# Shifted fp16 terms with GpSimd adds in place of every third VectorE exp pair of an attention and feed-forward kernel

## The chip, the cores and the metric

The kernel runs on one core of one Trainium2 chip. The metric is the device time of one execution in microseconds (us), median over runs. The engines are PE (TensorE; PEld is its weight load), ACT (ScalarE), DVE (VectorE), POOL (GpSimd) and SP, which issues the DMAs. All fast runs of one kernel here lie within 1.5% of each other, and all runs used below were in the fast state, except the two single runs that only price instructions, whose state is unknown.

## The reference, cut to what matters

```python
xn = layernorm(x)                                  # x: 1 x 2048 x 512, bf16
q = xn @ wq  (32 heads of 16);  k = xn @ wk;  v = xn @ wv   # one k and v for all heads
p = softmax(q @ k.T / 4)                           # 32 x 2048 x 2048 scores
s = (p @ v) @ wo
g = silu((silu(xn @ w_gate) * (xn @ w_up)) @ w_down)
return x + s * g
```

The exps dominate: 32 x 2048 x 2048 of them, in 1024 tiles of 128 x 1024.

## The kernel before

The kernel computes transposed scores into three PSUM slots of 128x1024 ("ring"), takes exps from two slots on ScalarE and from the third on VectorE, and multiplies them by the values into one accumulating PSUM bank ("o_ps"). Each engine's order of instructions is laid down at build time by a planner in the kernel, which simulates the engines with a duration for each operation. At run time each engine works strictly in that order and waits on semaphores.

VectorE's way to an exp needs no table. A score, scaled so that one unit is 1/1024 of an octave, is written as a uint16 whose bits, read as fp16, are a number near the exp (linear between powers of two). Two score tiles make a pair. A three-instruction tail turns the pair into two better terms, each with a value matmul of its own:

```python
# first pass, one for each of the two tiles; reads PSUM
pa = OP("DVE", 1.135, [...], nc.vector.tensor_scalar(out=Ub[ui][:, x*1024:(x+1)*1024], in0=ring[2][:],
        scalar1=ubias, scalar2=UINF, op0=ALU.add, op1=ALU.min))
# ... (cut: bookkeeping of the pair)
o1 = OP("DVE", 0.6, ..., out=Wb, in0=Ub, 0x3FF, 0x3800, bitwise_and, bitwise_or)      # mask
o2 = OP("DVE", 0.6, ..., out=Eb, in0=Ub, 0x7C00, bitwise_and)                         # exponent
o3 = OP("DVE", 1.135, ..., tensor_tensor(out=Wb, in0=Wb, in1=Ub, op=mult))            # product
# two value matmul groups per pair: Eb with VD[0], Wb with VD[1]
```

The second argument of `OP` is the planner's duration. Code is cut and shortened here.

Of the kernel before, what the change touches and what calls it, by code (L numbers as in the profile page):

```python
# [1 line left out]

# [8 lines left out]
FP16 = mybir.dt.float16  # L11
# [14 lines left out]
COFF = 4.0  # L26
CE, CW = 0.66858732, 0.66372796 * 1.0
DEN_LO = 16.0
# [5 lines left out]
PB_URG, AHEAD, LAZY, ACTMIN, ACTLOW = 6, 16, 8, 1.7, 1.5  # L34
TOL, MERGE = 0.12, 0.1

# [145 lines left out]
class _Sched:  # L182
    LAT = {"PE": 0.205, "ACT": 0.22, "DVE": 0.25, "POOL": 0.16, "DMA": 0.0, "EXT": 0.0}
    SAME = {"PE": 0.0, "ACT": 0.0, "DVE": 0.1, "POOL": 0.05, "DMA": 0.0}
    SWITCH = 0.105
    HOT = 0.3

    def __init__(self):
        self.free = {"PE": 0.0, "ACT": 0.0, "DVE": 0.0, "POOL": 0.0, "DMA": 0.0}
        self.ready = {e: [] for e in self.free}  # L190
        self.done = []
        self.pe_log = []
        self.seq = 0
        self.mode = None
        self.key = lambda o: o.prio
# [31 lines left out]
    def switch(self, mode):  # L227
        return self.SWITCH if self.mode is not None and mode != self.mode else 0.0

    def pick(self, e):  # L230
        lst = self.ready[e]
        if not lst:
            return None
        if e == "DMA":
            op = min(lst, key=lambda o: (o.ready, o.seq))
            return op.ready, op
        t = self.free[e]
        tm = max(t, min(o.ready for o in lst))
        now = [o for o in lst if o.ready <= tm + 1e-9]
        best = min(now, key=lambda o: (self.key(o), o.seq))  # L240
        if e == "DVE":
            hot = [o for o in lst if o.ready > tm and self.key(o)[0] < 1.6 and self.key(o) < self.key(best)]
            if hot:
                h = min(hot, key=lambda o: (o.ready, o.seq))
                fit = [o for o in now if tm + o.dur <= h.ready + self.HOT]
                best = min(fit, key=lambda o: (self.key(o), o.seq)) if fit else h
        return max(t, best.ready), best

    def place(self, op, start):
        e = op.eng  # L250
        op.start = start
        if e == "PE":
            op.start += self.switch(op.mode)
            self.mode = op.mode
        op.end = op.start + op.dur
        if e != "DMA":
            self.free[e] = op.end
        self.done.append(op)
        if e == "PE":
            self.pe_log.append(op)  # L260
        for u in op.users:
            u.left -= 1
            if u.left == 0:
                self._arm(u)
# [7 lines left out]
def kernel(  # L272
# [79 lines left out]
    vf = sb([P, NT, DH], FP32, "vf")  # L352
    VD = sb([P, 2, NT, 3 * DH], FP16, "VD")
    stats = sb([P, NT, nc.vector.BN_STATS_DIM], FP32, "stats")
    mv = sb([P, NT, nc.vector.BN_AGGR_DIM], FP32, "mv")
# [4 lines left out]
    QB = [sb([P, 512], BF16, f"QB{i}") for i in range(2)]  # L360
    NPB, NU, NE = 8, 3, 2
    Pb = [sb([P, 1024], BF16, f"Pb{i}") for i in range(NPB)]
    XB = [g2_sb[:, 2 * i:2 * i + 2, :].rearrange("p n d -> p (n d)") for i in range(NT // 2)]
    Ub = [sb([P, 2048], U16, f"Ub{i}") for i in range(NU)]
    Eb = [sb([P, 2048], U16, f"Eb{i}") for i in range(NE)]
    Wb = [sb([P, 2048], U16, f"Wb{i}") for i in range(NE)]
    th = [sb([P, 512], FP32, f"th{i}") for i in range(1)] * 2
# [120 lines left out]
    MMF = 0.215  # L488
    NBLK = NSC * NQ * 2
    NTILE = NBLK * NT * 2  # L490
    NPAIR = NSC * NQ
# [14 lines left out]
    def pro_x(c, pr, banks, ev_eng):  # L506
# [3 lines left out]
        for n0 in range(4 * c, 4 * c + 4, step):  # L510
# [22 lines left out]
            for n in range(n0, n0 + step):  # L533
                xo = OP("DVE", 0.33, [r, xr_rel[n % 4]], lambda n=n: e_xn(n), (pr - 0.15 if c == 0 else pr - 0.05, n),
                        name="xn")
                bk = banks[n % 4 // pk]
                h = n % pk
                t_ = OP("PE", 0.26, [xo, brel[bk]] + grp, lambda n=n, bk=bk, h=h: e_tr(n, bank[bk], h), (pr, n), "f",
                        "tr")
                xr_rel[n % 4] = t_  # L540
                grp = grp + [t_]
                if len(grp) == pk:
                    ee = ev_eng if n not in (1, 3) else "DVE"
                    ev = OP(ee, 0.5 if ee == "ACT" else 0.34 if pk == 1 else 0.6, grp,
                            lambda n=n, bk=bk, ee=ee: e_txe(n + 1 - pk, pk, bank[bk], ee), (pr - 0.1, n), name="txe")
                    if c:
                        held.append((grp[0], ev, bk))
                    grp = []
                    brel[bk] = ev
                    evs.append(ev)  # L550
# [24 lines left out]

    held = []
    evs = pro_x(0, 0.3, ("0a", "0b", "1a", "1b"), "ACT")
# [20 lines left out]
    for c in range(1, NSC):  # L598
# [7 lines left out]
        pro_v(c, evs, "2a", 0.7 + 0.01 * c)  # L606
    d_gate = [brel["2a"], brel["2b"], brel["m"]]

    m_rel = [brel["m"]]
# [63 lines left out]
    def e_out_add(n, src, eng):  # L673
        r = res[n % 4]
        return eng.tensor_tensor(out=r[:, :D], in0=src[:, :D], in1=x_sb[:, n, :], op=ALU.add)

# [3 lines left out]
    def g_out(n):  # L680
# [6 lines left out]
        m_rel[0] = m_  # L687
        ad = OP("POOL", 1.3, [m_, xr_rel[n % 4]], lambda: e_out_add(n, ab[i], nc.gpsimd), (0,), name="oadd")
        ab_rel[i] = ad
# [75 lines left out]
    unp = [[[], []] for _ in range(NBLK)]  # L765
    cur = {"ba": 0, "lastx": 1, "nA": 0, "exp": None, "pair": None, "np": 0, "issued": 0, "lastsc": None, "junk": 0, "nX": 0}
    slot = [None, None, None]
    pb_rel, w_rel, e_rel, wop_rel = [], [], [], []
    open_block(0)
# [126 lines left out]

    def act_sc(i, b, x, start):
        sc, t = place_sc(i, b, x, start, MMF)
        cur["lastx"] = x
# [11 lines left out]
        if k >= NPB:  # L911
# [3 lines left out]
                (1,), name="exp")  # L915
        cur["exp"] = ex
        slot[i] = ex
        unp[b][x].append((ex, k, t, buf))
# [16 lines left out]

    def dve_sc(b, x, start, dur):
        sc, t = place_sc(2, b, x, start, dur)
        first = cur["pair"] is None
        u = cur["np"]
        ui = u % NU  # L940
        pa = OP("DVE", 1.135, [sc, wop_rel[u - NU] if u >= NU else None],
                lambda: nc.vector.tensor_scalar(out=Ub[ui][:, x * 1024:(x + 1) * 1024], in0=ring[2][:], scalar1=ubias,  # L942
                                                scalar2=UINF, op0=ALU.add, op1=ALU.min), (1.5, u), name="passA")
        slot[2] = pa
        if first:
            cur["pair"] = (b, x, t, pa)
            return
        _, x0, t0, pa0 = cur["pair"]
        cur["pair"] = None
        cur["np"] += 1  # L950
        pair_blk.append(b)
        half = b % 2
        tx = {x0: t0, x: t}
        ei = u % NE
        o1 = OP("DVE", 0.6, [pa, pa0, w_rel[u - NE] if u >= NE else None], lambda: nc.vector.tensor_scalar(  # L955
            out=Wb[ei][:], in0=Ub[ui][:], scalar1=0x3FF, scalar2=0x3800, op0=ALU.bitwise_and,
            op1=ALU.bitwise_or), (2, u, 0), name="dM")
        o2 = OP("DVE", 0.6, [pa, pa0, e_rel[u - NE] if u >= NE else None], lambda: nc.vector.tensor_scalar(  # L958
            out=Eb[ei][:], in0=Ub[ui][:], scalar1=0x7C00, scalar2=None, op0=ALU.bitwise_and), (2, u, 1), name="dE")
        o3 = OP("DVE", 1.135, [o1, o2], lambda: nc.vector.tensor_tensor(  # L960
            out=Wb[ei][:].bitcast(FP16), in0=Wb[ei][:].bitcast(FP16), in1=Ub[ui][:].bitcast(FP16), op=ALU.mult),
            (2, u, 2), name="dW")
        wop_rel.append(o3)
        for i, (buf, o, rel) in enumerate(((Eb[ei], o2, e_rel), (Wb[ei], o3, w_rel))):
            mms = []
            dps = [o, oev[b - 1]]
            for g in range(4):
                tt = tx[g // 2]
                mms += mm_of(VD[:, i], lambda g, buf=buf: buf[:].bitcast(FP16)[:, g * 512:(g + 1) * 512], tt, half, (g,))
                dps.append(v_ready[tt // 4][i + 1])  # L970
            pv = OP("PE", MMF, dps, pv_emit(b, mms), (1, b, cur["nA"]), "c", "dpv")
            rel.append(pv)
            blk_pv[b].append(pv)
        check_done(b)
# [10 lines left out]
    LB = NBLK - 1  # L985
    LN = 4 * (NSC - 1)

# [99 lines left out]
    def pe_pick():  # L1087
# [42 lines left out]
        if tm is not None:  # L1130
            if ts is None or tm + sd.switch(co.mode) + co.dur <= ts + TOL:
                cands.append(tm)
            else:
                tm = None
        if td is not None and (ts is None or td + sd.switch("r") + MMF <= ts):
            if tm is None or td < tm - 0.2:
# [31 lines left out]
    def pe_do(start, what):  # L1168
# [20 lines left out]
        if kind == "dve":  # L1189
            dve_sc(arg[0], arg[1], start, MMF)  # L1190
            return
# [16 lines left out]
        if dt is not None and tile_ready(*dt) is not None:  # L1208
            at = max(sd.free["PE"], sd.avail(slot[2], "PE"), tile_ready(*dt))
            dve_sc(dt[0], dt[1], at, 0.015 if dt[1] != x else MMF)  # L1210

# [118 lines left out]
```

## Time and profile before

| | before |
|---|---|
| time, median | 788.7 us (786.6 to 790.0, 3 runs) |
| ACT busy, of a span of 786.6 us | 757.7 us, 96% |
| DVE busy | 740.2 us, 94% |
| PE busy | 723.8 us, 92% |
| POOL busy | 48.7 us, 6% |
| exps on ACT / first passes on DVE / tails on DVE | 778 / 246 / 123 |

From the page of the kernel before, the busy time of each engine and the groups of instructions that matter. The columns of a group are: line, engine, operation, output and input, form, count, then busy time and mean ns of one, then the engine's idle time just ahead of them and who ended it.

```profile
PE 723.8 (92%) x8097; PEld 218.6 (28%) x8098; DVE 740.2 (94%) x925; ACT 757.7 (96%) x864; POOL 48.7 (6%) x59
...
L914 ACT ACTIVATE Pb<-ring 128x1024 bf16<-128x1024 f32 x770 | 729.5, 1171 | 9.3 <-PE ring L856 8.6
L856 PE MATMUL ring<-QB,KT 32*128 32x512 bf16 x2048 | 319.0, 382 | 41.9 <-ACT Pb L914 35.3
L942 DVE TENSOR_SCALAR Ub<-ring 128x1024 uint16<-128x1024 f32 x246 | 299.3, 1217 | 12.3 <-PE ring L856 7.4
L960 DVE TENSOR_TENSOR Wb<-Wb,Ub 128x2048 f16<-128x2048 f16 x123 | 151.1, 1229 | 0.0
L958 DVE TENSOR_SCALAR Eb<-Ub 128x2048 uint16<-128x2048 uint16 x123 | 87.2, 714 | 0.0
```

Three engines are over 90% busy, and shares alone do not say which one bounds the kernel. Two stretches in mid-kernel do (the stretch and its length in us; then the busy us of PE, PEld, DVE, ACT and POOL in this order, with the number of instructions in brackets; then granted PE clock, DMA share, GB/s):

```profile
400.00:500.00 100.00, 92.29 (x1030) 27.78 (x1029) 98.29 (x118) 99.97 (x115) 7.18 (x6) 1.00 0.06 15
500.00:600.00 100.00, 93.79 (x1072) 27.22 (x1070) 95.95 (x112) 99.81 (x114) 2.98 (x2) 1.00 0.06 14
```

ACT has hardly a gap, DVE and PE have small ones. The waits agree (waiting us in total, times, longest):

```profile
ACT Pb L914 <- PE ring L856: 8.6, 13, 1.5
PE ring L856 <- ACT Pb L914: 35.3, 97, 1.0
```

ACT waited 8.6 us in the whole run for scores; PE waited four times that for ACT. So ACT is the bound, with DVE and PE close behind it.

### The profile page before, as it was taken

The numbers are of one execution on the slowest core, as the hardware profiler recorded it, in microseconds if no ns is written. First come the engines' busy times: TensorE is split into PE (matmuls) and PEld (weight loads), VectorE is DVE, ScalarE is ACT, GpSimd is POOL, SyncE is SP. The second block draws the span as 40 slices with busy tenths as digits, with TensorE's granted clock in tenths as the row PEclk, the third lists the DMA queues.
The fourth block names the chain that finished last, engine by engine and source line by source line (L and its number), as shares of the span: only waits on it lengthen the run. The fifth ranks groups of instructions, "written<-read, shape, count | busy, mean of one in ns | idle before, by whom it ended". The sixth has DMA issues, their size and how long they took to land.

```text
span 786.6 us, 19520 instructions
## 1 busy us (share of the span) xinstructions
PE 723.8 (92%) x8097; PEld 218.6 (28%) x8098; DVE 740.2 (94%) x925; ACT 757.7 (96%) x864; POOL 48.7 (6%) x59
## 2 busy tenths in 40 slices
PE   8999899999999899999999999989999999999995
PEld 3332232222222222222222222222222222222221
DVE  7678999999899999999999999999999999999997
ACT  6899899999999999999999999999999999999993
POOL 2100000000011000001002000000001100000001
PEclk9999999999899999999999999999999999999998
DMA  9300000000000000000000000000001000000001
GB/s 328 116 3 7 17 3 23 2 9 15 2 23 29 23 2 3 22 2 23 2 10 29 15 23 2 10 15 9 17 2 29 23 22 3 4 20 2 23 2 32
DMA packets 19464, 18.50 MB, mean 24 GB/s; under 512 B 8552, under 2 KB 15464, under 8 KB 19368
## 3 DMA queue, kind: packets, MB, share of 16 engines
q1 hardware_dynamic: 17496, 16.37, 6.9%
q8 instruction: 65, 1.06, 0.6%
q10 hardware_dynamic: 1872, 0.82, 0.4%
q14 instruction: 31, 0.25, 0.1%
HBM read 12.62 MB, written 2.34 MB: 19 GB/s over the span
## 4 chain that ended last, share of the span: by engine, by line
PE 36%; ACT 33%; DVE 20%; issue 9%; DMA 1%; SPq 0%; POOL 0%; ACTq 0%; DVEq 0%
ACT Pb L914 27%; PE ring L856 15%; PE m_ps L474 13%; PE o_ps L726 7%; DVE Ub L942 7%; ACT th L637 4%; DVE Wb L960 4%; DVE Eb L958 3%; DVE Wb L955 2%; ACT th L654 1%; DVE hT L643 1%; DVE ab L639 1%; DVE oa L739 1%; DMA dn<-oa 1%; DMA x_sb<-in_A_x_dram 0%
## 5 line engine op out<-in xcount | busy, mean ns | idle before, releaser
L914 ACT ACTIVATE Pb<-ring 128x1024 bf16<-128x1024 f32 x770 | 729.5, 1171 | 9.3 <-PE ring L856 8.6
L856 PE MATMUL ring<-QB,KT 32*128 32x512 bf16 x2048 | 319.0, 382 | 41.9 <-ACT Pb L914 35.3
L942 DVE TENSOR_SCALAR Ub<-ring 128x1024 uint16<-128x1024 f32 x246 | 299.3, 1217 | 12.3 <-PE ring L856 7.4
L856 PEld LDWEIGHTS <-KT 32*128 32x128 bf16 x2048 | 106.3, 90 | 349.7 <-issue 345.0
L960 DVE TENSOR_TENSOR Wb<-Wb,Ub 128x2048 f16<-128x2048 f16 x123 | 151.1, 1229 | 0.0
L726 PE MATMUL o_ps<-Pb,VA 128*32 128x512 bf16 x1540 | 149.1, 387 | 0.1
L958 DVE TENSOR_SCALAR Eb<-Ub 128x2048 uint16<-128x2048 uint16 x123 | 87.2, 714 | 0.0
L955 DVE TENSOR_SCALAR Wb<-Ub 128x2048 uint16<-128x2048 uint16 x123 | 86.0, 700 | 0.3 <-PE o_ps L726 0.2
L474 PE MATMUL m_ps<-xnT,wg_sb 128*32 128x512 bf16 x896 | 74.0, 384 | 0.8 <-DVE g_sb L656 0.3
L474 PE MATMUL m_ps<-wd_sb,hT 128*32 128x512 bf16 x896 | 73.4, 391 | 0.0
L474 PE MATMUL m_ps<-xnT,wu_sb 128*32 128x512 bf16 x896 | 70.7, 388 | 0.9 <-DVE ab L639 0.8
L711 POOL TENSOR_TENSOR oT<-oa,rb 128x512 bf16<-128x512 f32 x15 | 21.3, 1420 | 607.6 <-DMA rb<-dscr 267.8
L726 PEld LDWEIGHTS <-VA 128*32 128x32 bf16 x1556 | 38.6, 94 | 54.6 <-issue 53.8
L726 PE MATMUL o_ps<-Eb,VD 128*32 128x512 f16 x492 | 48.3, 386 | 2.6 <-DVE Eb L958 2.2
L726 PE MATMUL o_ps<-Wb,VD 128*32 128x512 f16 x492 | 48.8, 386 | 1.8 <-DVE Wb L960 1.2
L637 ACT ACTIVATE th<-m_ps 128x512 f32<-128x512 f32 x56 | 42.4, 758 | 0.0
L726 PEld LDWEIGHTS <-VD 128*32 128x32 f16 x984 | 29.0, 93 | 43.2 <-issue 41.2
L643 DVE TENSOR_TENSOR hT<-ab,m_ps 128x512 bf16<-128x512 f32 x56 | 38.1, 680 | 2.4 <-PE m_ps L474 2.1
L639 DVE SCALAR_TENSOR_TENSOR ab<-th,m_ps 128x512 f32<-128x512 f32 x56 | 38.0, 678 | 1.5 <-ACT th L637 1.0
L474 PEld LDWEIGHTS <-wg_sb 128*32 128x32 bf16 x896 | 17.2, 94 | 26.9 <-issue 26.3
L474 PEld LDWEIGHTS <-wu_sb 128*32 128x32 bf16 x896 | 16.4, 95 | 26.7 <-issue 24.5
L739 DVE COPY oa<-o_ps 128x512 f32<-128x512 f32 (+1 forms) x33 | 22.0, 668 | 1.5 <-PE o_ps L726 1.5
(106 smaller groups left out, 245.8 us busy)
## 6 DMA issues: line engine op xcount, KB each, us to landing
rb<-dscr SPq DMA_DIRECT2D x15, 256.0 KB
dn<-oa SPq DMA_DIRECT2D x120, 2.0 KB, 1.7
oa<-oa SPq DMA_DIRECT2D x60, 32.0 KB, 2.0
wg_sb<-in_B_w_gate_dram SPq DMA_DIRECT2D x1, 1792.0 KB, 12.1
wu_sb<-in_B_w_up_dram SPq DMA_DIRECT2D x1, 1792.0 KB
wd_sb<-in_B_w_down_dram SPq DMA_DIRECT2D x1, 1792.0 KB, 20.0
out_dram<-xn SPq DMA_DIRECT2D x14, 128.0 KB, 2.0
x_sb<-in_A_x_dram SPq DMA_DIRECT2D x3, 512.0 KB
```

The lines of the kernel that those rows point to most:

```text
L474: return [nc.tensor.matmul(out=dst[GRP * j:GRP * j + GRP, :], lhsT=w[:, GRP * j:GRP * j + GRP], rhs=rhs, start=start, stop=stop, tile_posi ...
L637: t_ = OP("ACT", 0.477, [a], lambda: nc.scalar.activation(out=th[i][:], in_=m_ps[:], func=ACT.Tanh, scale=0.5), (0,), name="tanh")
L639: s_ = OP("DVE", 0.6, [t_, ab_rel[i]], lambda: nc.vector.scalar_tensor_tensor(out=ab[i][:], in0=th[i][:], scalar=1.0, in1=m_ps[:], op0=ALU ...
L643: h = OP("DVE", 0.6, [b], lambda: nc.vector.tensor_tensor(out=hT[:, f, :], in0=ab[i][:], in1=m_ps[:], op=ALU.mult), (1,), name="hmul")
L726: r.append(nc.tensor.matmul(out=o_ps[GRP * g:GRP * g + GRP, :], lhsT=lhs, rhs=rhs, start=(n == 0), stop=(n == pv_total[(b, g)] - 1), tile_ ...
L739: oev[b] = sd.new(_Op("DVE", 0.6, [], lambda: [nc.vector.tensor_copy(out=oat[:, a:z], in_=o_ps[:, a:z]) for a, z in cuts], (0.2,), name="o ...
L856: return lambda: [nc.tensor.matmul(out=ring[sl][:, u * 512:(u + 1) * 512], lhsT=KT[half][GRP * g:GRP * g + GRP, t * P:(t + 1) * P], rhs=QB ...
L914: lambda: nc.scalar.activation(out=buf, in_=ring[i][:], func=ACT.Exp, scale=escale, bias=ebias),
L942: lambda: nc.vector.tensor_scalar(out=Ub[ui][:, x * 1024:(x + 1) * 1024], in0=ring[2][:], scalar1=ubias, scalar2=UINF, op0=ALU.add, op1=AL ...
L955: o1 = OP("DVE", 0.6, [pa, pa0, w_rel[u - NE] if u >= NE else None], lambda: nc.vector.tensor_scalar(out=Wb[ei][:], in0=Ub[ui][:], scalar1 ...
L958: o2 = OP("DVE", 0.6, [pa, pa0, e_rel[u - NE] if u >= NE else None], lambda: nc.vector.tensor_scalar(out=Eb[ei][:], in0=Ub[ui][:], scalar1 ...
L960: o3 = OP("DVE", 1.135, [o1, o2], lambda: nc.vector.tensor_tensor(out=Wb[ei][:].bitcast(FP16), in0=Wb[ei][:].bitcast(FP16), in1=Ub[ui][:]. ...
```

## The change

The intent is to free VectorE, so that it can take more exp tiles from ScalarE, by using idle GpSimd. Every third pair has no tail. Instead the first pass is followed on POOL by three adds of 256, 512 and 768 to the uint16 bits, a quarter octave each; the four fp16 numbers, weighted in the values by powers of 2^(-1/4), sum to a good exp. The pair then needs four value matmul groups instead of two. To find room, seven scratch buffers and eight rows of x that are dead after the layer norm form one pool of nine, other x rows hold the new value weights, and x is loaded again for the output add. The planner gets rules that keep POOL and VectorE's SBUF passes apart.

```diff
+K4 = (0.24037645, 0.20213265, 0.16996992, 0.14292964)
+KOFF = 256.0
+DPRI, DTOL, DWIN = 1.2, 0.12, 0.15
-TOL, MERGE = 0.12, 0.1
+TOL, MERGE, KE, KB = 0.17, 0.1, 3, 3.0
@@ planner: POOL operations and DVE's SBUF passes exclude each other
+    LOCKS = ("dM", "dE", "dW", "xn")
+        if e == "POOL" or e == "DVE" and op.name in self.LOCKS:
+            self.lock[e] = op.end
@@ buffers
-    Ub = [sb([P, 2048], U16, f"Ub{i}") for i in range(NU)]      (Eb and Wb likewise)
+    Bf = [sb([P, 2048], U16, f"Bf{i}")[:] for i in range(7)]
+    Bf += [x_sb[:, 4 * c:4 * c + 4, :].rearrange("p n d -> p (n d)").bitcast(U16) for c in range(2)]
@@ a pair in shifted terms
+        if k4:
+            for i in range(3):
+                bi, brl = kb[i]
+                kadd.append(OP("POOL", 1.0, [pa] + brl, lambda i=i, bi=bi: nc.gpsimd.tensor_scalar(
+                    out=Bf[bi][:, hs], in0=U[:, hs], scalar1=KOFF * (i + 1), scalar2=0.0,
+                    op0=ALU.add, op1=ALU.add), (2, u), name="kadd"))
@@ its value matmuls
+            terms.append((ui, [pa, pa0], VD[:, 0], None, 1))
+            for i in range(3):
+                terms.append((kb[i][0], [kadd[i], kadd0[i]], VK[i], [vk_ready[i]], 0))
@@ the output add
+        ld = OP("DMA", 2.2, ..., dma_start(out=res[n % 4][:, :D], in_=x_v[:, n, :]))
... (cut: making the value weights, buffer choice, the score-issue rules that use DPRI, DTOL, DWIN)
```

The built order of the changed kernel has 768 exps on ACT, 256 first passes and 86 tails on DVE, 42 pairs in shifted terms (252 adds on POOL), and 8442 matmuls where there were 8097.

## The prediction

The prediction was made without running the change:

> **What bounds the kernel now.** The page gives three nearly full engines over 786.6 us: ACT 96%, DVE 94%, PE 92%; POOL 6%. The table by stage decides: from 400 to 770 us ACT is busy 99.8 to 100 of every 100 us, with about 104 exps (0.935 us each) and 10 tanhs (0.75 us). In the waits, exps wait 8.6 us in total, all for PE; PE's score matmuls wait 35.3 us for ACT, 3.3 us for DVE. So ACT is the bound: 778 exps, 72 tanhs, and 29 us of idle, mostly prologue and tail. DVE and PE are close behind, PE with some 40 us of slack.
>
> **What the change does (by the built order of instructions).**
> - ACT: 778 exps become 768.
> - DVE: 246 first passes (1.22 us) become 256, but 37 of 123 three-instruction tails (mask, exponent, multiply; about 2.4 us at their pitch) go; 42 of 128 pairs are shifted terms. Estimate: +11 - 88 = -77 us, from 740 to about 665 us.
> - POOL: 252 adds of 128x1024 uint16, an op the trace lacks. Estimate from its one-input ops (128 elements 0.302 us, 512 elements 0.611 us: 0.8 ns per element plus 0.2 us): 1.05 us each, 265 us in all; POOL goes to about 310 us.
> - PE: a shifted pair needs four value matmul groups instead of two; 8097 matmuls become 8442, at about 0.055 us each (eight in 0.43 us) +19 us. Runs of 12 column matmuls between two scores go from 43 to 150; such a run takes about 1.13 us from score to score (8 take 0.91 us) against ACT's 0.935 us.
> - x reloads: 12 small DMAs off the path.
>
> **POOL against DVE.** At 324.4 us a 0.7 us exponent pass took 1.41 us while POOL ran, and the multiply, median 1.2 us, reached 2.0 us. The Trainium skill, "SBUF — State Buffer", section "Who interferes with whom", says that the second to issue blocks fully until the first finishes; this trace agrees. The new scheduler keeps them apart in its plan. I expect 20 to 50 us of blocked time in all, absorbed by DVE's freed 77 us.
>
> **On the critical path.** Only the ten exps: 10 x 0.935 = 9.4 us. The DVE saving mostly becomes slack. PE loses about half its slack, and ACT sometimes gets its score late (longer column runs, value matmuls queued behind a late POOL add): I allow +1 to 2 us of ACT waits net. 788.7 - 9.4 + 1.7 = 781 us.
>
> **Predicted 781 us, 8 in 10 between 771 and 794.** Chances: faster by over 2% 0.11, within 2% 0.83, slower by over 2% 0.06.
>
> **What would show each step right or wrong.**
> - ACT still fullest, 96% or more, exps x768 at an unchanged 0.935 us.
> - DVE busy 650 to 690 us, its idle time growing; first pass still 1.22 us.
> - The POOL add's shortest time about 1.05 us, some near 1.7 us (blocked); POOL 280 to 340 us busy.
> - PE busy about 740 us; score matmuls' wait for ACT shrinks from 35 to 15 to 25 us.
> - ACT's wait for scores grows from 8.6 us to 10 to 20 us.
> - PE's value matmuls wait less than 10 us for POOL.
>
> **What would make it wrong.** The POOL add being 1.6 us or more: terms come late, PE stalls in order, ACT starves, and the time passes 794. POOL and DVE drifting into each other so that passes run late: same result. ACT waits vanishing with PE keeping up: then about 772. A false dependence between the exp buffers and value weights that share the x tile: waits between PE, POOL and DVE on that tile.

Its price for the POOL add came from the groups of one-input POOL operations in the kernel before. This is the reading:

```profile
L470 POOL TENSOR_SCALAR VD<-vf 128x128 f16<-128x128 f32 x8 | 2.3, 302 | 0.0
L411 POOL COPY wk_rep<-wk_sb 128x512 bf16<-128x512 bf16 x1 | 0.6, 611 | 2.8 <-DMA wk_sb<-in_A_wk_dram 2.8
```

And its reading of the conflict between POOL and DVE came from the timeline (start us, length us, engine, line). The exponent pass takes 0.68 us in the median of its 123, and here 1.41 us beside a POOL operation:

```profile
323.97 1.27 POOL L711 TENSOR_TENSOR oT<-oa,rb 128x512 bf16<-128x512 f32 x1 [47.52 <-DMA rb<-dscr]
324.38 1.41 DVE L958 TENSOR_SCALAR Eb<-Ub 128x2048 uint16<-128x2048 uint16 x1
```

## The result, and the profile after

Ratios here and below are the mean time of one kernel's fast runs over the mean of the other's fast runs of the same rounds, which is not quite the ratio of the medians quoted.

| | before | after |
|---|---|---|
| time, median | 789.3 us (4 runs) | 1341.4 us (1339.1 to 1349.2, 4 runs) |
| ratio | | 1.701, 95% interval 1.691 to 1.711 |
| ACT busy, share of span | 757.7 us, 96% | 777.4 us, 58% |
| DVE busy | 740.2 us, 94% | 717.6 us, 54% |
| POOL busy | 48.7 us, 6% | 997.2 us, 74% |
| mean granted PE clock | 0.99 | 0.745 |

The page after: busy times, the granted clock in 40 slices (tenths), and groups.

```profile
PE 910.0 (68%) x8442; PEld 224.3 (17%) x8443; DVE 717.6 (54%) x824; ACT 777.4 (58%) x854; POOL 997.2 (74%) x317
...
PEclk9975786777767777778776787767867577777787
...
L951 ACT ACTIVATE Pb<-ring 128x1024 bf16<-128x1024 f32 x760 | 736.3, 1050 | 538.0 <-PE ring L891 520.8
L1018 POOL TENSOR_SCALAR Bf<-Bf 128x1024 uint16<-128x1024 uint16 x182 | 686.9, 3793 | 214.5 <-DVE Bf L1010 174.1
L1010 DVE TENSOR_SCALAR Bf<-ring 128x1024 uint16<-128x1024 f32 x208 | 253.7, 1220 | 336.8 <-PE ring L891 305.9
```

One POOL add takes 3.79 us in the mean, not 1.05 us. The first pass on DVE (1.22 us) is unchanged. The exps do the same work, but ACT idles 538 us ahead of them. The chain that ended last, by engine and then by line:

```profile
POOL 65%; PE 16%; issue 12%; DVE 4%; ACT 2%; DMA 1%; SPq 0%; POOLq 0%; DVEq 0%; ACTq 0%
POOL Bf L1018 53%; POOL x_sb L1018 10%; PE o_ps L760 5%; PE ring L891 5%; PE m_ps L493 4%; DVE Bf L1010 2%; POOL oT L745 1%; ACT Pb L951 1%; POOL xn L708 1%; ACT g_sb L951 0%; DVE x_sb L1010 0%; DMA oa<-oa 0%; DMA x_sb<-in_A_x_dram 0%; DMA rb<-dscr 0%; DVE xnT L463 0%
```

Before, POOL had 0% of that chain. The waits say how the add reaches ACT:

```profile
ACT Pb L951 <- PE ring L891: 520.8, 236, 10.5
PE o_ps L760 <- POOL Bf L1018: 341.4, 91, 10.5
DVE Bf L1010 <- PE ring L891: 305.9, 85, 14.2
POOL Bf L1018 <- DVE Bf L1010: 174.1, 22, 14.7
```

PE's value matmuls wait 341.4 us for POOL on this line and 44.6 us on adds into the x rows, 386.0 us in all. PE works in order, so scores for ACT that stand behind such a matmul wait too: ACT waits 520.8 us for scores, where it had waited 8.6 us. Then DVE waits for its scores, and POOL for DVE: a ring in which nobody is full, as these two stretches show.

```profile
400.00:500.00 100.00, 68.93 (x616) 15.99 (x613) 58.77 (x61) 59.70 (x65) 73.46 (x20) 0.72 0.03 7
1000.00:1100.00 100.00, 69.56 (x580) 15.70 (x580) 50.19 (x54) 55.25 (x60) 77.50 (x25) 0.67 0.04 10
```

One such event, first PE, then POOL, then ACT (start us, length us, engine, line, and in brackets the idle time just before, with who ended it). PE issues a value matmul on an unshifted term, then stands for 8.55 us in front of the first shifted term:

```profile
301.67 0.40 PE L760 MATMUL o_ps<-Bf,VD 128*32 128x512 f16 x4
310.61 0.62 PE L760 MATMUL o_ps<-Bf,VK 128*32 128x512 f16 x4 [8.55 <-POOL Bf L1018]
311.16 0.61 PE L891 MATMUL ring<-QB,KT 32*128 32x512 bf16 x2
```

```profile
302.97 4.00 POOL L1018 TENSOR_SCALAR x_sb<-Bf 128x1024 uint16<-128x1024 uint16 x1
306.94 7.22 POOL L1018 TENSOR_SCALAR Bf<-Bf 128x1024 uint16<-128x1024 uint16 x2
```

```profile
295.13 7.73 ACT L951 ACTIVATE Pb<-ring 128x1024 bf16<-128x1024 f32 x8 [0.50 <-PE ring L891]
311.87 1.02 ACT L951 ACTIVATE Pb<-ring 128x1024 bf16<-128x1024 f32 x1 [9.01 <-PE ring L891]
```

The idle time in brackets is 8.55 us on PE and 9.01 us on ACT. The value matmul could start when the add that began at 306.94 had ended, 3.6 us later. Four matmuls took 0.40 us before the wait and 0.62 us after it. The Trainium skill, "TensorE: Matmul & The Clock Gate", section "Part 1: The HAM clock gate (the "warmup" mystery)", says that the clock is halved after about 3.4 us of idle PE. The trace agrees: in this wait PE's last matmul ended at about 302.07 us, and the granted clock was 1.00 from 302 to 304 us, 0.92 from 304 to 306 us and 0.50 from 306 us on. In the 100 us stretches from 100 us on it was 0.67 to 0.80, where before it was 0.97 or more in mid-kernel. The low clock is read here as a consequence of the idling. The same matmuls in the same order were busy 724.5 us in run 4 below and 910.0 us here, so it lengthened PE's work by 186 us; how much of the loss that makes up was not separated.

### The profile page after: what moved, and what is told of

It is laid out like the page before. It is cut to its first block, busy times and chain, and to the rows that moved or that the text cites. A ratio compares the mean times of both kernels' runs of the same rounds, so it can differ in the third digit from the quotient of the medians.

```text
span 1340.5 us, 20409 instructions
## 1 busy us (share of the span) xinstructions
PE 910.0 (68%) x8442; PEld 224.3 (17%) x8443; DVE 717.6 (54%) x824; ACT 777.4 (58%) x854; POOL 997.2 (74%) x317
## 4 chain that ended last, share of the span: by engine, by line
POOL 65%; PE 16%; issue 12%; DVE 4%; ACT 2%; DMA 1%; SPq 0%; POOLq 0%; DVEq 0%; ACTq 0%
POOL Bf L1018 53%; POOL x_sb L1018 10%; PE o_ps L760 5%; PE ring L891 5%; PE m_ps L493 4%; DVE Bf L1010 2%; POOL oT L745 1%; ACT Pb L951 1%; POOL xn L708 1%; ACT g_sb L951 0%; DVE x_sb L1010 0%; DMA oa<-oa 0%; DMA x_sb<-in_A_x_dram 0%; DMA rb<-dscr 0%; DVE xnT L463 0%
## 5 line engine op out<-in xcount | busy, mean ns | idle before, releaser
L951 ACT ACTIVATE Pb<-ring 128x1024 bf16<-128x1024 f32 x760 | 736.3, 1050 | 538.0 <-PE ring L891 520.8
L1018 POOL TENSOR_SCALAR Bf<-Bf 128x1024 uint16<-128x1024 uint16 x182 | 686.9, 3793 | 214.5 <-DVE Bf L1010 174.1
L1010 DVE TENSOR_SCALAR Bf<-ring 128x1024 uint16<-128x1024 f32 x208 | 253.7, 1220 | 336.8 <-PE ring L891 305.9
L891 PE MATMUL ring<-QB,KT 32*128 32x512 bf16 x2048 | 369.3, 453 | 19.7 <-ACT Pb L951 13.5
L1018 POOL TENSOR_SCALAR x_sb<-Bf 128x1024 uint16<-128x1024 uint16 x40 | 150.8, 3771 | 40.7 <-DVE Bf L1010 40.7
L760 PE MATMUL o_ps<-Bf,x_sb 128*32 128x512 f16 x280 | 53.3, 573 | 162.6 <-POOL Bf L1018 162.6
L1018 POOL TENSOR_SCALAR Bf<-x_sb 128x1024 uint16<-128x1024 uint16 x28 | 105.7, 3796 | 25.6 <-DVE x_sb L1010 22.0
L1010 DVE TENSOR_SCALAR x_sb<-ring 128x1024 uint16<-128x1024 f32 x48 | 58.5, 1220 | 82.0 <-PE ring L891 74.1
L760 PE MATMUL o_ps<-Bf,VD 128*32 128x512 f16 x652 | 74.6, 445 | 3.9 <-DVE oa L773 1.9
L760 PEld LDWEIGHTS <-x_sb 128*32 128x32 f16 x336 | 15.1, 102 | 232.7 <-issue 232.4
L1044 DVE TENSOR_TENSOR Bf<-Bf,Bf 128x2048 f16<-128x2048 f16 x41 | 52.1, 1271 | 0.0
L1042 DVE TENSOR_SCALAR Bf<-Bf 128x2048 uint16<-128x2048 uint16 x53 | 47.3, 892 | 0.0
```

The lines of the kernel that those rows point to most:

```text
L760: r.append(nc.tensor.matmul(out=o_ps[GRP * g:GRP * g + GRP, :], lhsT=lhs, rhs=rhs, start=(n == 0), stop=(n == pv_total[(b, g)] - 1), tile_ ...
L891: return lambda: [nc.tensor.matmul(out=ring[sl][:, u * 512:(u + 1) * 512], lhsT=KT[half][GRP * g:GRP * g + GRP, t * P:(t + 1) * P], rhs=QB ...
L951: lambda: nc.scalar.activation(out=buf, in_=ring[i][:], func=ACT.Exp, scale=escale, bias=ebias),
L1010: lambda: nc.vector.tensor_scalar(out=U[:, hs], in0=ring[si][:], scalar1=bias, scalar2=UINF, op0=ALU.add, op1=ALU.min), (1.5, u), name="pa ...
L1018: kadd.append(OP("POOL", 1.0, [pa] + brl, lambda i=i, bi=bi: nc.gpsimd.tensor_scalar(out=Bf[bi][:, hs], in0=U[:, hs], scalar1=KOFF * (i + ...
L1042: o2 = OP("DVE", 0.6, [pa, pa0] + erel, lambda: nc.vector.tensor_scalar(out=Bf[ei], in0=U, scalar1=0x7C00, scalar2=None, op0=ALU.bitwise_a ...
```

## The experiments

Theories, named as in the expectations:

- A: the add is slow by itself, 3.6 us where the plan (1.0) and the prediction (1.05) had a third of it, and the late terms stop PE, then ACT.
- B: the add is quick, but conflicts with DVE stretch it.
- C: scratch buffers and value weights that share the x tile wait for each other needlessly.
- D: the new order rules (longer column runs between scores) are what costs.

### 1. Pricing POOL forms

Edit, at the idle end of the kernel before:

```diff
+    for _ in range(3):   # 14 more groups like this, with other types, sizes and operations
+        nc.gpsimd.tensor_scalar(out=B_, in0=A_, scalar1=256.0, scalar2=0.0, op0=ALU.add, op1=ALU.add)
     MAIN.close()
```

> The kernel before, with groups of three POOL instructions each appended at its end, when all other engines are idle; their results are not used. Theory A (the uint16 add is slow by itself): the 128x1024 uint16 add takes about 3.6 us here too, with nothing to conflict with, about 3.3 ns per element above a small constant, so 512 columns take about 1.9 us and 128 columns about 0.6 us. Theory B (the adds are stretched by conflict with VectorE): here it takes about 1.05 us. Which property is slow (integer type, two operations, arithmetic) is read from the other forms; I expect the same form in float32 or float16 at about 1.0 to 1.1 us, and a packed int32 add of two tensors, 128x512, at about 1.3 us, as the float32 two-tensor forms of the kernel before take 1.2 to 1.3 us.

In the groups of this run, L1303 is add-add on 1024 uint16 columns, L1305 add alone, L1307 and L1309 add-add on 512 and 128 columns, L1313 multiply-add on 1024 fp16 columns, L1315 add-add in float32.

```profile
L1303 POOL TENSOR_SCALAR Wb<-Ub 128x1024 uint16<-128x1024 uint16 x3 | 10.9, 3635 | 0.3
L1305 POOL TENSOR_SCALAR Wb<-Ub 128x1024 uint16<-128x1024 uint16 x3 | 8.3, 2770 | 0.2
L1307 POOL TENSOR_SCALAR Wb<-Ub 128x512 uint16<-128x512 uint16 x3 | 5.8, 1925 | 0.2
L1309 POOL TENSOR_SCALAR Wb<-Ub 128x128 uint16<-128x128 uint16 x3 | 1.9, 641 | 0.2
L1313 POOL TENSOR_SCALAR Wb<-Ub 128x1024 f16<-128x1024 f16 x3 | 3.1, 1044 | 0.2
L1315 POOL TENSOR_SCALAR Wb<-Ub 128x1024 f32<-128x1024 f32 x3 | 10.9, 3628 | 0.2
```

Add-add takes 3.63 us with all other engines idle, in uint16, float32, fp16 and int16 alike. From 128 to 1024 columns it grows by (3635 - 641) / 896 = 3.34 ns per element. Multiply-add takes 1.04 us. Theory B falls, and so does my guess that the type decides: float32 was expected at 1.0 to 1.1 us. What differs is the pair of operations. The packed int32 add of two tensors took 1.26 us (1.3 expected), and 1.04 us with the second one a broadcast constant.

The prediction's price was taken from L470, which is a multiply-add, and from a copy. Both are quick forms. It was carried over to an add-add, of which the trace had no example.

### 2. Which pairs are quick

The same method with nine groups, add-add among them once more.

> The kernel before with groups of three POOL instructions appended at the idle end: which pair of operations is quick on 128x1024 uint16. Expected: multiply-add 1.04 us; multiply-subtract, multiply-multiply and the add-multiply unknown, 3.6 us if only multiply-add is quick; one operation alone (multiply, subtract) 2.8 us as add alone was; add-add again 3.63 us; multiply-add in float32 1.04 us.

Multiply-add (L1303), add-then-max (L1307) and multiply alone (L1309), 1024 uint16 columns:

```profile
L1303 POOL TENSOR_SCALAR Wb<-Ub 128x1024 uint16<-128x1024 uint16 x3 | 3.1, 1047 | 0.3
L1307 POOL TENSOR_SCALAR Wb<-Ub 128x1024 uint16<-128x1024 uint16 x3 | 10.9, 3634 | 0.2
L1309 POOL TENSOR_SCALAR Wb<-Ub 128x1024 uint16<-128x1024 uint16 x3 | 8.3, 2776 | 0.2
```

| operations | us |
|---|---|
| multiply-add (also float32), add-multiply, multiply-multiply | 1.05 |
| one operation alone: multiply, subtract (and add, in the run above) | 2.77 to 2.78 |
| add-add, add-max, multiply-subtract | 3.63 |

The expectation left some pairs open; the odd part is that multiply-add is quicker than multiply alone.

### 3. The change without its shifted terms

```diff
-        return cur["np"] % KE == 0 and planned(vk_ready) and ...
+        return False and cur["np"] % KE == 0 and planned(vk_ready) and ...
```

> The changed kernel with the shifted-term pairs switched off; nine buffers in dead x rows, the x reloads and the new order rules stay. 780 exps on ScalarE, 244 first passes, 122 tails. Theory A: 785 to 800 us, within 2% of before. Theory C (the cost comes from false waits between buffers that share the x tile) or D (the new order rules): well over 820 us, with VectorE or PE waits on the x tile.

785.9 us median, ratio to before 0.995 (0.988 to 1.003), correct. With the pool of nine buffers, the x reloads and the new rules in place, nothing is lost. The order rules and the buffer pool by themselves are not the cause. The value weights in x rows are made but not used here, so this alone does not close theory C.

### 4. The same order and waits, but short adds

```diff
-  out=Bf[bi][:, hs], in0=U[:, hs], scalar1=KOFF * (i + 1), ...
+  out=Bf[bi][:, x * 1024:x * 1024 + 240], in0=U[:, x * 1024:x * 1024 + 240], scalar1=KOFF * (i + 1), ...
```

> The changed kernel with the same order of instructions on every engine and the same waits, but each POOL add only over the first 240 of 1024 columns, which should take about 1.0 us, the time its planner assumed; the result is wrong on purpose. Theory A: 773 to 795 us, as predicted for the change, PE waits for POOL under 20 us. Theories C and D: still over 1000 us, since the dependences and the order are unchanged.

785.3 us, ratio 0.995 (0.989 to 1.002); the result is wrong. The median add took 1.02 us, and PE waited 3.7 us for POOL, not 386 us:

```profile
PE o_ps L760 <- POOL Bf L1018: 3.7, 3, 2.1
```

The buffers and their tile, the order and the dependences were those of the changed kernel. Theories C and D fall: the short adds take away the whole of the loss (1341.4 - 785.3 = 556 us). They are shorter in time and in bytes at once; run 7 separates the two.

### 5. Half as many slow pairs

```diff
-        return cur["np"] % KE == 0 and planned(vk_ready) ...
+        return cur["np"] % KE == 0 and cur.get("nk", 0) < 21 and planned(vk_ready) ...
```

> The changed kernel with its slow add-add form, but only 21 shifted-term pairs instead of 42. Theory A: each pair costs its six adds in turn, (1341 - 786) / 42 = 13.2 us per pair, so 786 + 21 x 13.2 = 1063 us, give or take 30. A cost that starts with the first late pair and then grows with the drift (a threshold) would give over 1150; one that comes mainly from later crowding less than 950.

1057.7 us (2 runs), expected 1063. The cost is 13 us per slow pair, as with 42 pairs; no threshold shows. The trace shows both regimes in one run, a stretch with slow pairs and one after the last of them:

```profile
500.00:600.00 100.00, 66.21 (x584) 15.45 (x587) 48.13 (x54) 54.17 (x59) 74.94 (x22) 0.72 0.03 8
900.00:1000.00 100.00, 92.22 (x1078) 27.75 (x1076) 96.86 (x114) 100.00 (x116) 3.62 (x2) 1.00 0.04 10
```

### 6. Packed int32 adds

```diff
-  nc.gpsimd.tensor_scalar(out=Bf[bi][:, hs], in0=U[:, hs], scalar1=KOFF * (i + 1), scalar2=0.0, op0=add, op1=add)
+  nc.gpsimd.tensor_tensor(out=Bf[bi][:, hs].bitcast(I32), in0=U[:, hs].bitcast(I32),
+                          in1=kc[:, i:i + 1].to_broadcast([P, 512]), op=add)     # kc = 65537 * 256 * (i + 1)
```

> The changed kernel in the same order, with each POOL add done as a two-tensor int32 add over 128x512 words, two uint16 values per word, the constant read through a broadcast; the result should stay right. Theory A: the add takes about 1.3 us, POOL about 360 us busy, and the time falls to 775 to 810 us; below 789 would beat the kernel before. Theories C and D: over 1000 us.

791.3 us, ratio 1.002 (0.994 to 1.009), correct; the median add took 1.04 us, less than the 1.3 us expected. The Trainium skill, "GPSIMD Engine Reference", section "4.1 Engine selection", says that such a 32-bit add is exact; the correct result agrees. It mends the change, but does not beat the kernel before.

### 7. Multiply by 1, then add

```diff
-  scalar1=KOFF * (i + 1), scalar2=0.0, op0=ALU.add, op1=ALU.add
+  scalar1=1.0, scalar2=KOFF * (i + 1), op0=ALU.mult, op1=ALU.add
```

> The changed kernel in the same order, with each POOL add written as multiply by 1, then add, instead of add, then add 0: the same value. The appended forms showed 1.04 us for multiply-add in float16 against 3.63 us for add-add in every type. Theory A: the uint16 add takes about 1.05 us, no run of it under 1.0 us, the result is right, and the time is 778 to 790 us, like the short adds (785), as I predicted for the change; its ratio to before 0.985 to 1.003. Theory A2 (multiply-add is quick only in float16): still 1341 us.

790.2 us, ratio 1.002 (0.999 to 1.006), correct. The add's shortest, median and longest ns over its largest group:

```profile
L1018 POOL TENSOR_SCALAR Bf<-Bf x182: 1036/1044/2021, 61.5 to 759.3; 128x1024 uint16<-128x1024 uint16 x182
```

Writing the same value with another pair of operations takes 551 us off the changed kernel. The bytes are those of the slow add, so it is the time of the add that costs. PE waited 3.9 us for POOL. The median duration came out as first predicted; the time is at the upper end of what was expected (778 to 790) and above the prediction's 781. Ten exps were taken from ACT, and no gain is left.

### 8. Where the ten exps went

First, the multiply-add kernel with adds over 16 columns (`hs` becomes 16 columns; wrong):

> As the multiply-add kernel, but each add over the first 16 of 1024 columns: about 0.2 us. Wrong on purpose. It prices what a POOL add of 1 us still costs (conflict with VectorE, late terms). Theory A with a conflict that VectorE's slack absorbs: 772 to 786 us, at most 8 us under the multiply-add kernel, VectorE's busy time about 660 us, down from 675 with the short adds. If the conflict weighs, more than 8 us lower.

780.4 us, ratio 0.993 (0.989 to 0.998). The difference from run 7 is 10 us by the medians, above the 8 us named. DVE's busy time was 670.2 us, against 697.7 us in run 7.

Is it drift of the plan? The planner was told 1.1 us instead of 1.0:

> The multiply-add kernel, with the planner told that a POOL add takes 1.1 us (three in a row took 3.30 us on the chip) instead of 1.0, so that its plan to keep POOL and VectorE apart fits the chip better. 770 exps, 85 tails, 42 shifted-term pairs. If the 10 us between the multiply-add and the tiny-add kernels come from drift of the plan: 778 to 784 us, VectorE's busy time down from 698 to under 685 us, ratio to before about 0.99. If the conflict is there whatever the planner knows: 785 to 792 us, VectorE's busy time 690 us or more.

794.6 us, ratio 1.005 (1.002 to 1.008), DVE busy 692.1 us. This is above both expected ranges. A truer duration did not help, so drift as the cause is not supported; but the plan also came out different (770 exps), so the run does not exclude it.

Is it the traffic, or the time that an add takes? Three kernels with one order, five rounds on one chip. Quiet adds are add-add over 256 columns, about as long as a full multiply-add but with a quarter of its bytes:

> Add-add over 256 columns: about 1.06 us per add, as long as the full multiply-add, but a quarter of its SBUF traffic. Wrong on purpose. If the conflict of traffic costs the 10 us: ratio to before near the tiny adds' (0.990 to 0.995), VectorE's busy time about 676 us. If the delay of terms costs them: near the full adds' (1.000 to 1.006).

> The multiply-add kernel again, on this chip: ratio to before 0.999 to 1.006, VectorE's busy time about 698 us.

> The tiny adds again, on this chip: ratio to before 0.988 to 0.996, VectorE's busy time about 670 us.

| | time, median | ratio to before (95%) | DVE busy | ACT's wait for scores |
|---|---|---|---|---|
| tiny adds | 778.9 us | 0.989 (0.986 to 0.992) | 669.8 us | 3.0 us |
| quiet adds | 785.3 us | 0.996 (0.992 to 1.000) | 677.1 us | 9.0 us |
| full adds | 791.5 us | 1.002 (0.998 to 1.006) | 697.3 us | 15.1 us |

The lines behind the two last columns, in the order of the table (page, then waits):

```profile
PE 724.1 (93%) x8442; PEld 215.5 (28%) x8443; DVE 669.8 (86%) x824; ACT 746.9 (96%) x854; POOL 133.9 (17%) x317
```

```profile
ACT Pb L951 <- PE ring L891: 3.0, 6, 1.1
```

```profile
PE 730.6 (93%) x8442; PEld 215.5 (28%) x8443; DVE 677.1 (86%) x824; ACT 749.0 (96%) x854; POOL 360.6 (46%) x317
```

```profile
ACT Pb L951 <- PE ring L891: 9.0, 15, 2.0
```

```profile
PE 736.5 (93%) x8442; PEld 216.0 (27%) x8443; DVE 697.3 (88%) x824; ACT 751.1 (95%) x854; POOL 359.5 (45%) x317
```

```profile
ACT Pb L951 <- PE ring L891: 15.1, 28, 1.6
```

Both seem to matter. An add that lasts 1 us costs about 6 us even with little traffic: every tiny-add run was faster than every quiet-add run, and the intervals are just apart (0.9919 and 0.9922). This is not delay alone, since DVE's busy time still rises by 7.3 us. Full traffic adds about 6 us more; there the intervals overlap a little, so that part is likely, not certain. In each step ACT's wait for scores, in the one profiled execution of each, grows by 6 us, about as much as the median time. Where PE finds each late input is spread over many short waits, and was not traced further.

### 9. Other numbers of shifted pairs

`KE` in the multiply-add kernel set to 4 and to 2:

> The multiply-add kernel with every fourth pair in shifted terms instead of every third: 31 pairs, 772 exps, 95 tails. If terms gain nothing net (exps saved are paid back in conflict): 785 to 791 us, as for every third. A gain would be under 783 us.

789.2 us, ratio 0.999 (0.995 to 1.003): no gain, within the 785 to 791 named for that.

> The same with every second pair: 65 pairs, 762 exps, 66 tails, POOL adds x390, about 410 us of POOL. Another six exps off ScalarE (5.6 us), but 20 us more value matmuls on PE, whose slack is by then nearly gone, and half as much conflict again: 788 to 802 us, ScalarE's waits for scores above the 12 us of every third. Only if ScalarE alone bounds it, under 785 us.

830.3 us, ratio 1.055 (1.049 to 1.060), correct, far above the 788 to 802 expected. Six exps fewer than with every third pair, and 40 us slower. ACT waited 22.9 us for scores, and 29.7 us ahead of tanhs for PE. More terms are worse than I had thought; the order was planned anew, so this is not only the price of the terms, and its cause was not traced.

### 10. A planner that knows the slow add

```diff
-  kadd.append(OP("POOL", 1.0, [pa] + brl, ...
+  kadd.append(OP("POOL", 3.65, [pa] + brl, ...
```

> The slow add-add form, with the planner told that it takes 3.65 us. It then makes 22 shifted-term pairs, 806 exps, 87 tails. If the 1341 us came from a wrong duration in the plan, and not from the work itself: 806 to 830 us, set by the 806 exps at 0.935 us (754 us) with tanhs and ends (80 us), PE's waits for POOL under 30 us. If the slow adds cost whatever the plan knows: near the 1058 us of the other kernel with 21 slow pairs.

919.5 us (2 runs), ratio 1.164 (1.158 to 1.170). The expectation missed. PE's wait for POOL is indeed small, but another wait is there:

```profile
ACT Pb L951 <- PE o_ps L760: 64.1, 21, 8.4
PE o_ps L760 <- POOL Bf L1018: 3.8, 2, 2.1
```

ACT now waits for value matmuls, and it makes 806 exps. Knowing the duration removes half of the harm: (919.5 - 786) / 22 = 6 us per slow pair, against 13 us, although ACT has 28 more exps than in the kernel before. Why ACT waits there was not tested; my reading is that exp buffers stay full while one accumulation bank waits for the late terms of a block.

## Why the prediction was wrong

1. **The bound.** ScalarE as the bound before: right. With tiny adds, so with the change's order but almost no POOL time, the time is 778.9 against 786.8 us, a gain of 7.9 us; the ten exps were priced at 9.4 us.
2. **The step that failed** is "POOL: 252 adds of 128x1024 uint16 ... Estimate from its one-input ops ...: 1.05 us each, 265 us in all". It measured 3.63 us alone and 3.79 us in the mean of its largest group. The estimate extended a multiply-add and a copy to an add-add, and runs 1 and 2 show that the pair of operations, not the type, makes the difference of 3.5 times. With multiply-add the step holds within 1%: 1.044 us median. The sum held less well: over all 252 adds, some of them up to 2.0 us long, the mean was 1.24 us, and POOL was busy 360 us, where about 310 us (280 to 340) was predicted.
3. **The consequence** was named under what would make the prediction wrong ("terms come late, PE stalls in order, ACT starves") and happened just so: 386 us of PE waiting for POOL, 521 us of ACT waiting for scores. It got little weight (0.06 for slower by over 2%), since the add's price was taken as known.
4. **Conflict of POOL and DVE.** Predicted 20 to 50 us of blocked time. The multiply-add kernel shows 698 - 670 = 28 us more DVE busy time than the tiny adds. But "absorbed by DVE's freed 77 us" was wrong in part: full adds lose 12 us against tiny ones, of which about half seems to come with the traffic. DVE's busy time has slack; a late result in an ordered stream has not.
5. **ACT waits.** "+1 to 2 us net" was mis-sized. With the add at its predicted price, ACT's waits for scores grew from 8.6 to 12.4 us (run 7) and 15.1 us (run 8), inside the 10 to 20 us that the prediction itself listed as a check; but all of ACT's idle time grew from 28.9 to 38.6 and 41.2 us (span less busy time), by 10 to 12 us. With tiny adds it was 29.1 us. So the corrected change ended at ratio 1.002 instead of the predicted 0.99.
6. **Right:** DVE busy 670 us without conflict (665 predicted), first pass unchanged at 1.22 us; with multiply-add, PE's value matmuls waited 3.9 us for POOL (under 10 predicted); no false dependence on the x tile, reloads without effect.

No version here is clearly faster than the kernel before. The best correct one, the change without its terms, has ratio 0.995 with an interval that includes 1.

## What to carry to other kernels

Price an operation from a trace only by the same form: engine, operation pair, size. If the trace has none, measure it at the idle end of a kernel first; that takes one run. Work moved to an idle engine is not free when its results enter another engine's strict order: one late term stops everything queued behind it, so price that delay, and the time in which POOL and DVE hold each other up, as well as the busy time.

## What the Trainium skill lacked or had wrong

- "GPSIMD Engine Reference", section "4.1 Engine selection", says of elementwise work that one-input operations are roughly line-rate. On 128x1024 that holds for multiply-add, add-multiply, multiply-multiply and a copy (1.04 to 1.05 us), not for a single add, subtract or multiply (2.77 us), nor for add-add, add-max and multiply-subtract (3.63 us).
- The same page, section "3.1 Elementwise — side-by-side cycle accounting", has 1.03 cycles per element for short bodies (at most two operations per element). Multiply-add agrees (0.302 us for 128 columns in the kernel before and 1.044 us for 1024 in run 1: 0.83 ns per element, one cycle at the page's 1.2 GHz). Add-add has 3.34 ns per element, four such cycles, though it too is two operations; no page gives a time for this pair.
- "SBUF — State Buffer", section "Who interferes with whom", says that when a DVE instruction in a 2-port mode meets a GpSimd instruction, the one that issues second is blocked for the whole of the other. With multiply-adds the trace agrees: in the full-adds run, 43 of the 44 mask and exponent passes on DVE that began inside an add ended 0.54 to 0.67 us after that add. With the slow add-add it does not: in the changed kernel, 80 of 114 such passes ended before the add did. It depends on how long the add still had to run. With 1.06 us or less left (34 passes), the pass ended 0.54 to 0.55 us after the add. With 1.5 to 2.7 us left (46 passes), it took 0.63 to 0.69 us, as when alone. With 2.8 us or more left (34 passes), it took 0.81 to 1.53 us. So an add-add held DVE up at its beginning and at its end, and not in between. This is read from start and end times alone; no run was built to test it. One pass of the middle kind, inside an add that ran from 189.57 to 193.63 us:

```profile
189.57 4.06 POOL L1018 TENSOR_SCALAR x_sb<-x_sb 128x1024 uint16<-128x1024 uint16 x1
191.79 0.68 DVE L1042 TENSOR_SCALAR Bf<-Bf 128x2048 uint16<-128x2048 uint16 x1
```

The quiet adds fit this: add-adds over 256 columns, 1.07 us long, left DVE busy 677 us, multiply-adds over 1024 columns, 1.04 us long, 697 us.
